# Re-ordering w_out's loads, batch 1's output and batches 2 and 3 around an expert block of an attention and gated-MLP kernel

## The chip, the cores and the metric

The kernel runs on one core of a Trainium2 chip. The core has several engines that work side by side, each through its own queue in order: TensorE (PE, matrix products, with a separate record PEld for loading weights), VectorE (DVE), ScalarE (ACT), GpSimd (POOL) and SyncE (SP, which here only issues DMAs). An instruction starts when the one before it on its engine is done and the semaphores it waits for are set. Loads are issued on POOL's queue and cast to fp16 on the way; DMA transposes and the stores are issued on SP. The metric is the device time of one execution in microseconds; lower is better. The median of three runs of the kernel before is 320.43 us (320.16 to 321.76).

## The reference, cut to what matters

```python
# q, k, v: (8 batches, 8 heads, 576 tokens, 64)
kv = einsum('bhsd,bhse->bhde', k, v)
o  = einsum('bhsd,bhde->bhse', q, kv)          # linear attention, no softmax
o  = o / sqrt(mean(o*o, axis=-1) + 1e-6) * g_norm
x  = o.transpose(0, 2, 1, 3).reshape(4608, 512)
ffn = (gelu(x @ w_gate) * (x @ w_val)) @ w_out    # w_gate, w_val: (512, 1536), w_out: (1536, 512)
out = x + sigmoid(x @ w_res) * ffn
```

Each batch is a small attention followed by an RMS norm per head; all 4608 tokens then go through a gated MLP with a gated residual. `mean(o*o)` is the sum of squares that the kernel calls `ss`, and the reciprocal of the root is its norm.

## The kernel before, in words

**Blocks and batches.** Tokens are handled in nine blocks. Block b, for b from 0 to 7, holds the first 512 tokens of batch b; block 8 holds the remaining 64 tokens of all eight. The MLP runs over d_ff in `NF` = 12 slices of 128 and over tokens in `NJ` = 4 groups of 128. `m_gval(blk, f)` computes one slice of gate and value (products of `xT`, the transposed normed tokens, with w_gate and w_val, tiles `gps` and `vps`), has ACT take the Gelu and DVE multiply the two into `hid`. For block 0 `out_by_f` multiplies `hid` with w_out slice by slice, f by f, four token groups each (`m_ffn`, tile `fps`). From block 1 on, the output is made by seven products of sums of quarters of `hid` and w_out (tiles `wA`, `wD`, `wE`, `wF`), a Strassen scheme; the sums of w_out are `wo_sums(0..3)` into `wo_ts`, those of `hid` `s_begin`, `s_rest` and `s_last`. Block 2 and later use such sums for gate and value as well (`weight_sums`, `token_sums`, tiles `Ag`, `Fg`, `Av`, `Fv`).

**Attention, one or two blocks ahead.** The attention of batch b is cut into steps which are put between pieces of the MLP of an earlier block: `load_batch` (loads of q, k, v on POOL), `by_token` (a copy of q that brings a token's heads together), `a_qT` or `d_qT` (transpose of q on PE or by DMA), `a_kv` (products of k and v into `kvp`, one copy out), `a_o` (32 small products into `op`), `a_ss` (square on ACT, reduction on DVE, one for each quarter), `a_norm` (the reciprocal root, on DVE or POOL), `a_t` (scaling `op` into `t`, DVE), `a_xT` or `d_xT` (transpose of t into `xT`, PE or DMA), and `a_g` or a scaled copy for g_norm.

**What sets the order.** The program is written out by hand: each block has a list of slots, and a dictionary `plan` from slot to steps that are issued behind it. In block 0, slots 0 to 11 are gate and value, 12 to 15 the residual gate (`m_res`, tile `rps`), 16 to 27 the output slices f = 0 to 11 (slot `NF + 4 + f`). Block 1 has `m_gval` f = 0 to 11 in slots 0 to 11, two slots of two residual products each (12 and 13), and then the seven products. `attn_plan_1` gives the steps of batch 1, which stand in block 0; `plan_attn_2` those of batch 2, in block 1; `plan_attn_ahead(b)` those of batch b in block b - 2 (batch 3 in block 1, beside batch 2). `aside_out(blk, word, ...)` puts steps between the seven products. The order on an engine is the order of issue in the program; no engine changes it.

**The loads in block 0.** Behind slot 2 POOL issues w_res, then batch 1's q, k, v and their last 64 rows (`kl`, `vl`), then w_out in four parts:

```python
load_batch(1)
for f0, f1 in ((0, 2), (2, 4), (4, 8), (8, NF)):
    load_wo(f0, f1)
```

The queue has eight DMAs in flight at most: each issue waits for the landing of one eight earlier, and the profile shows that wait before each w_out issue (1.8 to 1.9 us).

**The holds.** `load_behind(b)` issues batch b + 1's loads on POOL behind a one-element copy (tile `hold`) from the transpose of q of batch b, so that loads do not run before that transpose is done:

```python
nc.gpsimd.tensor_copy(out=hold, in_=st[b]["qT"][0:1, 0, 0, 0:1])
if x_of is not None:
    nc.gpsimd.tensor_copy(out=hold, in_=xT_t[x_of][0:1, 0, 0, 0:1])
```

Everything else that POOL has to do later waits behind that copy and the issues, the norm of batch 3 among it.

Of the kernel before, what the change touches and what calls it, by code (L numbers as in the profile page):

```python
# [18 lines left out]
def kernel(  # L19
# [96 lines left out]

    def load_batch(b):
        tiles_16(b)
        raw[b, "q"] = stage.tile([P, H, NJ * D], FP16, tag="qraw", name="qraw")
        nc.gpsimd.dma_start(out=raw[b, "q"], in_=rows4(q, b, 0, H))  # L120
        nc.gpsimd.dma_start(out=b16_t[b, "k"], in_=rows4(k, b, 0, H))
        nc.gpsimd.dma_start(out=b16_t[b, "v"], in_=rows4(v, b, 0, H))
        load_last_kv(b)
        if pair(b) is not None:
            load_qr(2 * pair(b))
            load_qr(2 * pair(b) + 1)

    def by_token(b, copy=nc.vector.tensor_copy, js=slice(0, NJ)):
# [169 lines left out]
    def a_norm(b, j0, j1, eng=nc.vector):  # L298

        s = st[b]  # L300
        if "rinv" not in s:
            s["rinv"] = attnp.tile([P, NJ + 1, H], FP32, tag="ny", name="ny")
        ss, yy = (t[:, j0:j1, :].rearrange("p j h -> p (j h)") for t in (s["ss"], s["rinv"]))
        n = (j1 - j0) * H
        m = attnp.tile([P, (NJ + 1) * H], FP32, tag="nm", name="nm")[:, 0:n]
        a = attnp.tile([P, (NJ + 1) * H], FP32, tag="na", name="na")[:, 0:n]
        mh = attnp.tile([P, (NJ + 1) * H], FP32, tag="nh", name="nh")[:, 0:n]
        magic = 0x5F1FFFF9 if eng is nc.gpsimd else 0x5F3759DF
        eng.tensor_scalar(out=m, in0=ss, scalar1=1.0 / D, scalar2=RMS_EPS, op0=ALU.mult, op1=ALU.add)
        eng.tensor_scalar(  # L310
            out=yy.bitcast(I32), in0=m.bitcast(I32), scalar1=-0.5, scalar2=float(magic), op0=ALU.mult, op1=ALU.add
        )
        if eng is nc.gpsimd:
            for step in range(2):
                eng.tensor_tensor(out=a, in0=yy, in1=yy, op=ALU.mult)
                eng.tensor_tensor(out=a, in0=a, in1=m, op=ALU.mult)
                c = (-0.703952253, 0.703952253 * 2.38924456) if step == 0 else (0.375, -1.25)
                eng.tensor_scalar(out=mh, in0=a, scalar1=c[0], scalar2=c[1], op0=ALU.mult, op1=ALU.add)
                if step == 1:
                    eng.tensor_tensor(out=mh, in0=mh, in1=a, op=ALU.mult)  # L320
                    eng.tensor_scalar(out=mh, in0=mh, scalar1=1.875, scalar2=None, op0=ALU.add)
                eng.tensor_tensor(out=yy, in0=mh, in1=yy, op=ALU.mult)  # L322
            return
        eng.tensor_scalar(out=mh, in0=m, scalar1=-0.5, scalar2=None, op0=ALU.mult)
        for _ in range(3):
            eng.tensor_tensor(out=a, in0=yy, in1=yy, op=ALU.mult)
            eng.tensor_tensor(out=a, in0=a, in1=mh, op=ALU.mult)
            eng.scalar_tensor_tensor(out=yy, in0=a, scalar=1.5, in1=yy, op0=ALU.add, op1=ALU.mult)

    def pair(b):  # L330

        return b - B // 2 if b >= B // 2 else None
# [16 lines left out]

    def a_xT(b, j):  # L350

        blk, jj = where(b, j)
        ps = pattn.tile([P, NP, P], FP16, tag="at", name="xtp")
        for cc in range(NP):
            nc.tensor.transpose(ps[:, cc, :], t_t[blk][:, jj, cc * P : (cc + 1) * P], ident)
        nc.scalar.activation(
            out=xT_t[blk][:, jj, :, :], in_=ps, func=AF.Copy, scale=gcol
        )

# [60 lines left out]

    def m_gval(blk, f, pool=pmoe, tag="mm"):
        if f == 0:
            hids[blk] = hidp.tile([P, NF, NJ * P], FP16, tag="hid", name="hid")
        gps = pool.tile([P, NJ * P], FP32, tag=tag, name="gps")
        m_mm(gps, wg_c, f, blk, 0, NJ)
        vps = pool.tile([P, NJ * P], FP32, tag=tag, name="vps")
        m_mm(vps, wv_c, f, blk, 0, NJ)
        m_act(blk, f, gps, vps)
# [491 lines left out]
    def gv_group(blk, g, banks, amid, order):  # L920
# [67 lines left out]
        for word in ORDERS[order].split():  # L988
# [12 lines left out]
            for f in amid.get(word, ()):  # L1001
                f()

    def out_by_f(blk):

# [9 lines left out]
        def step(f):  # L1015
# [3 lines left out]
            for j in range(NJ):  # L1019
                m_ffn(blk, j, f, fpss[j])  # L1020
            if NFH <= f < NFH + NJ:
                m_sigmoid(f - NFH)
# [301 lines left out]
    def attn_plan_1():  # L1324
# [11 lines left out]
                lambda: load_batch(b + 1),  # L1336
                lambda: a_kv(b),
                *[lambda j=j: a_x(0, j) for j in range(NJ)],
            ],
            NF + 4: [lambda: a_o(b), ss[0], ss[1]],  # L1340
            NF + 5: [ss[2], ss[3]],
            NF + 6: [lambda: a_norm(b, 0, NJ), t[0], t[1], t[2], t[3]],
            2 * NF: [x[0], x[1]],
            2 * NF + 1: [x[2]],
            2 * NF + 2: [x[3], lambda: wo_sums(0), lambda: wo_sums(2)],
        }
        return plan

# [20 lines left out]
    def plan_attn_2():  # L1369
# [5 lines left out]
        at(m, 3, lambda: load_behind(b))  # L1375
        at(m, 1, lambda: wo_sums(1))
        at(m, 3, lambda: wo_sums(3))
        at(m, 4, lambda: a_o(b))
        for j in range(NJ):
            at(m, 4 + j // 2, lambda j=j: a_ss(b, j))  # L1380
        at(m, 6, lambda: a_norm(b, 0, NJ, nc.gpsimd))
        for j in range(NJ):
            at(m, 9 + j // 2, lambda j=j: a_t(b, j))
        at(m, 10, lambda: d_xT(b, 0, NJ))
# [14 lines left out]
    def plan_attn_ahead(b):  # L1399
# [22 lines left out]
        else:  # L1422
            at(m, 8, lambda: by_token(b, act, slice(0, 2)))
            at(m, 9, lambda: by_token(b, act, slice(2, 4)), *begin)
            at(m, NF - 1, lambda: a_kv(b, act))
            at(m, NF, lambda: load_behind(b))
        if rem:
# [7 lines left out]
        else:  # L1435
            at(m, NF, lambda: a_o(b), lambda: a_ss(b, 0), lambda: a_ss(b, 1))
            aside_out(m, "D", lambda: a_ss(b, 2), lambda: a_ss(b, 3))
# [28 lines left out]
    sums = {u: weight_sums(u, nc.vector) for u in units}  # L1466
    for slot, u in ((2, ("g", 1)), (4, ("g", 2)), (NF - 1, ("v", 1))):
        for i in range(2):
            at(0, slot + i, *sums[u][2 * i : 2 * i + 2])
    at(0, 6, *sums["v", 2][0:2])  # L1470
    at_word(0, 0, "1v", *sums["v", 2][2:4])
    late_sums = [f for u in (("g", 0), ("v", 0)) for f in sums[u]]
    for i, f in enumerate(late_sums[0:6]):
        at(1, (2, 6, 7)[i // 2], f)
    aside_out(1, "D", *late_sums[6:8])
# [52 lines left out]
    for blk in range(B + 1):  # L1528
# [21 lines left out]
        else:  # L1550
# [27 lines left out]
            if blk == 1:  # L1578
                slots[0] = lambda: m_gval(1, 0, pattn, "at")
            outs = []  # L1580
            slots += [lambda i=i: outs[i]() for i in range(4 if blk < B else 2)]
            if not groups:
                plan.setdefault(NFH + 2, []).insert(0, lambda: s_begin(blk))

# [20 lines left out]
        for s in range(len(slots)):  # L1605
# [4 lines left out]
            if blk == 0 and s == 2:  # L1610
                nc.gpsimd.dma_start(out=wr16, in_=moe_w_res.rearrange("(cc p) c -> p cc c", p=P))
                load_batch(1)
                for f0, f1 in ((0, 2), (2, 4), (4, 8), (8, NF)):
                    load_wo(f0, f1)
# [33 lines left out]
```

## Time and profile before

| What | Value |
|---|---|
| Median of three runs | 320.43 us |
| Lowest and highest | 320.16 and 321.76 us |
| Profiled execution, device time | 321.37 us |
| Its span in the trace | 319.6 us |
| Granted PE clock, mean | 0.997 |
| PE busy | 309.9 us, 97% |
| DVE busy | 274.4 us, 86% |
| ACT busy | 210.4 us, 66% |
| POOL busy | 188.1 us, 59% |
| DMA moved | 38.89 MB |

The profiled execution is 0.94 us above the median; its span leaves out 1.77 us of its device time. A row of a timeline gives the start in us from the span's start, the duration, the engine, the line, the operation, what it writes and reads, its shape, and in brackets the idle time of the engine just before it with what ended that idle time. Rows of one kind that follow each other are joined, so "x32" are 32 instructions. Matmuls overlap their neighbours, so their durations are longer than their distances: four of 512 columns in a row are 0.865 us apart from the next four. The table of waits names, for each line of an engine, the engine or load that it waited for.

### The profile page before, as it was taken

The numbers are of one execution on the slowest core, as the hardware profiler recorded it, in microseconds if no ns is written. First come the engines' busy times: TensorE is split into PE (matmuls) and PEld (weight loads), VectorE is DVE, ScalarE is ACT, GpSimd is POOL, SyncE is SP. The second block draws the span as 40 slices with busy tenths as digits, with TensorE's granted clock in tenths as the row PEclk, the third lists the DMA queues.
The fourth block names the chain that finished last, engine by engine and source line by source line (L and its number), as shares of the span: only waits on it lengthen the run. The fifth ranks groups of instructions, "written<-read, shape, count | busy, mean of one in ns | idle before, by whom it ended". The sixth has DMA issues, their size and how long they took to land.

```text
span 319.6 us, 7763 instructions
## 1 busy us (share of the span) xinstructions
PE 309.9 (97%) x3039; PEld 246.3 (77%) x3039; DVE 274.4 (86%) x488; ACT 210.4 (66%) x385; POOL 188.1 (59%) x248
## 2 busy tenths in 40 slices
PE   8899989999999999999999999999999999999992
PEld 3544755444788888888888888888888888888882
DVE  5886979799898999989998999899988777897774
ACT  4763675455848794879587858695767467836760
POOL 2873350573769478856885888517851375396331
PEclk9999999999999999999999999999999999999998
DMA  7999999999994699479967794800540003001104
GB/s 254 327 174 198 198 200 199 177 159 184 162 130 82 199 134 111 72 216 127 108 82 216 90 143 79 216 8 0 53 162 2 0 3 134 0 2 56 77 0 131
DMA packets 77381, 38.89 MB, mean 122 GB/s; under 512 B 42274, under 2 KB 75042, under 8 KB 77346
## 3 DMA queue, kind: packets, MB, share of 16 engines
q0 software_dynamic: 39280, 17.17, 42.8%
q1 hardware_dynamic: 37488, 20.71, 25.9%
q8 instruction: 23, 0.38, 0.5%
q10 hardware_dynamic: 578, 0.52, 0.5%
q14 instruction: 12, 0.10, 0.1%
HBM read 38.80 MB, written 9.44 MB: 151 GB/s over the span
## 4 chain that ended last, share of the span: by engine, by line
PE 84%; DMA 11%; SPq 1%; POOL 1%; DVE 1%; issue 0%; DVEq 0%
PE Av L949 12%; PE Ag L949 12%; PE wA L518 11%; PE Fv L949 6%; PE Fg L949 6%; DMA wg<-in_moe_w_gate_dram 5%; DMA wo<-in_moe_w_out_dram 5%; PE rA L569 4%; PE gps L413 3%; PE fps L450 3%; PE vps L413 3%; PE Eg L949 3%; PE wF L518 3%; PE wE L518 3%; PE wD L518 3%; PE Ev L949 3%
## 5 line engine op out<-in xcount | busy, mean ns | idle before, releaser
L986 POOL TENSOR_TENSOR hid<-ge,c 128x512 f16<-128x512 f16 x22 | 25.6, 1165 | 37.3 <-ACT ge L980 35.9
L518 PEld LDWEIGHTS <-hid_s 128*128 128x128 f16 x384 | 37.6, 98 | 4.3
L364 POOL TENSOR_TENSOR t<-t,g 128x512 f16<-128x512 f16 x32 | 37.8, 1212 | 0.0
L949 PEld LDWEIGHTS <-wsv 128*128 128x128 f16 x352 | 34.1, 98 | 4.8 <-issue 0.3
L949 PEld LDWEIGHTS <-wsg 128*128 128x128 f16 x352 | 34.4, 98 | 4.0
L705 POOL TENSOR_TENSOR osb<-osb,t 128x512 f32<-128x512 f32 x28 | 34.1, 1249 | 0.0
L959 ACT COPY Eg<-Ag 128x512 f32<-128x512 f32 x22 | 12.8, 582 | 27.9 <-PE Ag L949 27.9
L518 PEld LDWEIGHTS <-hid 128*128 128x128 f16 x288 | 28.2, 98 | 3.5
L949 PEld LDWEIGHTS <-wg 128*128 128x128 f16 x264 | 25.8, 98 | 3.2
L949 PEld LDWEIGHTS <-wv 128*128 128x128 f16 x264 | 25.8, 98 | 3.0
L949 PE MATMUL Av<-ts,wsv 128*128 128x256 f16 x176 | 26.4, 272 | 0.1
L949 PE MATMUL Ag<-ts,wsg 128*128 128x256 f16 x176 | 26.4, 273 | 0.0
L970 DVE TENSOR_TENSOR Fg<-Ag,d 128x512 f32<-128x512 f32 x22 | 15.3, 696 | 11.1 <-ACT d L963 8.2
L261 DVE TENSOR_REDUCE ss<-sq 128x8 f32<-128x512 f32 x32 | 20.5, 679 | 2.3 <-ACT sq L256 2.3
L401 ACT ACTIVATE ge<-gps 128x512 f16<-128x512 f32 x20 | 11.8, 597 | 15.5 <-PE gps L413 14.8
L518 PE MATMUL wA<-wo_ts,hid_s 128*128 128x256 f16 x168 | 20.6, 272 | 0.0
L348 DVE TENSOR_TENSOR t<-op,ny 128x512 f16<-128x512 f32 x28 | 18.7, 684 | 1.0 <-POOL ny L322 0.4
L980 ACT ACTIVATE ge<-Eg 128x512 f16<-128x512 f32 x22 | 13.1, 597 | 9.2 <-PE Eg L949 9.2
L413 PE MATMUL vps<-xT,wv 128*128 128x512 f16 x72 | 18.5, 379 | 0.4 <-DMA wv<-in_moe_w_val_dram 0.3
L980 ACT ACTIVATE ge<-c 128x512 f16<-128x512 f32 x22 | 13.8, 625 | 7.7 <-DVE c L970 7.7
L413 PE MATMUL gps<-xT,wg 128*128 128x512 f16 x72 | 18.5, 379 | 0.0
L980 ACT ACTIVATE ge<-Fg 128x512 f16<-128x512 f32 x22 | 13.0, 591 | 8.3 <-PE Fg L949 6.6
(220 smaller groups left out, 852.5 us busy)
## 6 DMA issues: line engine op xcount, KB each, us to landing
out_dram<-osb SPq DMA_DIRECT2D x14, 512.0 KB, 3.8
qraw<-in_q_dram POOLq DMA_DIRECT2D x7, 512.0 KB, 6.7
k<-in_k_dram POOLq DMA_DIRECT2D x7, 512.0 KB, 8.4
v<-in_v_dram POOLq DMA_DIRECT2D x7, 512.0 KB, 11.0
wg<-in_moe_w_gate_dram POOLq DMA_DIRECT2D x2, 512.0 KB, 9.3
wo<-in_moe_w_out_dram POOLq DMA_DIRECT2D x2, 512.0 KB, 13.7
out_dram<-osb SPq DMA_DIRECT2D x4, 256.0 KB, 3.7
wv<-in_moe_w_val_dram POOLq DMA_DIRECT2D x3, 256.0 KB, 8.4
```

The source lines that it names most:

```text
L261: nc.vector.tensor_reduce(out=out_, in_=sqs.pop((b, i)), op=ALU.add, axis=mybir.AxisListType.X)
L348: nc.vector.tensor_tensor(out=t, in0=o, in1=scale, op=ALU.mult)
L364: eng.tensor_tensor(out=t_t[blk][:, jj, :], in0=t_t[blk][:, jj, :], in1=g16, op=ALU.mult)
L413: nc.tensor.matmul(ps[:, j0 * P : j1 * P], lhsT=w[:, cc, :], rhs=xT_t[blk][:, j0:j1, cc, :], start=(cc == 0 and j0 == 0), stop=(cc == NP - ...
L518: nc.tensor.matmul(ps[:, e - es[0], :], lhsT=a[:, f, e * P : (e + 1) * P], rhs=b[:, f, :], start=(start and e == es[0] and f == 0), stop=( ...
L569: nc.tensor.matmul(out_[:, e, :], lhsT=x_[:, e, cc, :], rhs=w_[:, cc, :], start=(first and e == 0 and cc == 0), stop=(cc == 1), skip_group ...
L705: nc.gpsimd.tensor_tensor(out=res_all[of], in0=res_all[of], in1=t_t[blk][of], op=ALU.add)
L949: nc.tensor.matmul(out_[:, r, :], lhsT=lhsT, rhs=rhs, start=(first and r == 0 and c == 0), stop=(c == 1), skip_group_check=True,)
L959: nc.scalar.copy(out=tile_of("E", u), in_=ps["A", u])
L970: nc.vector.tensor_tensor(out=dst, in0=ps["A", u], in1=sb["d", u], op=ALU.add)
L980: nc.scalar.activation(out=ge[q], in_=source(q, "g"), func=AF.Gelu)
L986: eng.tensor_tensor(out=dst, in0=ge[q], in1=source(q, "v"), op=ALU.mult)
```

## The change

- **w_out's loads.** Slices 0 to 2 are issued between k and v of batch 1, then slice 3, then 4 and 5, 6 to 8 and 9 to 11 behind batch 1's loads: five parts for four.
- **`load_batch`.** It takes `amid`, what to issue between k and v; the remainders' `qr` loads go ahead of k; for batch 4 the last rows of k and v are issued later, at the end of block 1's products.
- **Batch 1.** `a_kv` moves from behind the residual products to behind f = 2 of block 0's output, with its copy on ACT for DVE; `a_o` and all four `ss` go into f = 3 behind its second token group (`amid_step`); norm and `t` go behind f = 4; the four `xT` go behind f = 10 and into f = 11, the third evacuated on DVE for ACT. `wo_sums(0)` and `wo_sums(2)` leave block 0 for block 1.
- **Norm on DVE.** Nine operations with other constants instead of twelve.
- **Block 1's first `m_gval`.** Both products of f = 0 are made in two halves of 256 columns.
- **Batch 2.** `a_o` and `ss` one slot later, the norm on DVE for POOL and one slot later, `t` one slot earlier; some sums of weights in other slots; `s_begin` of block 1 in slot 10 for 8.
- **Batch 3.** `a_kv` one slot later (behind the first two residual products), `a_o` one slot later (behind all four), and batch 4's loads are held for batch 2's `xT` as well as batch 3's `qT`.

The order of DMAs on SP is the same in both kernels: batch 3's transpose of q is issued ahead of batch 2's transpose of x in both.

```diff
-    def load_batch(b):
+    def load_batch(b, amid=lambda: None):
...
-        nc.gpsimd.dma_start(out=b16_t[b, "k"], in_=rows4(k, b, 0, H))
-        nc.gpsimd.dma_start(out=b16_t[b, "v"], in_=rows4(v, b, 0, H))
-        load_last_kv(b)
         if pair(b) is not None:
             load_qr(2 * pair(b))
             load_qr(2 * pair(b) + 1)
+        nc.gpsimd.dma_start(out=b16_t[b, "k"], in_=rows4(k, b, 0, H))
+        amid()
+        nc.gpsimd.dma_start(out=b16_t[b, "v"], in_=rows4(v, b, 0, H))
+        if pair(b) != 0:
+            load_last_kv(b)
...
-        eng.tensor_scalar(out=mh, in0=m, scalar1=-0.5, scalar2=None, op0=ALU.mult)
-        for _ in range(3):
-            eng.tensor_tensor(out=a, in0=yy, in1=yy, op=ALU.mult)
-            eng.tensor_tensor(out=a, in0=a, in1=mh, op=ALU.mult)
-            eng.scalar_tensor_tensor(out=yy, in0=a, scalar=1.5, in1=yy, op0=ALU.add, op1=ALU.mult)
+        eng.tensor_tensor(out=a, in0=yy, in1=yy, op=ALU.mult)
+        eng.tensor_tensor(out=a, in0=a, in1=m, op=ALU.mult)
+        eng.scalar_tensor_tensor(out=mh, in0=a, scalar=2.38924456, in1=yy, op0=ALU.subtract, op1=ALU.mult)
+        eng.tensor_tensor(out=a, in0=mh, in1=mh, op=ALU.mult)
+        eng.tensor_tensor(out=a, in0=a, in1=m, op=ALU.mult)
+        eng.scalar_tensor_tensor(
+            out=yy, in0=a, scalar=1.25 / (0.375 * c**2), in1=a, op0=ALU.subtract, op1=ALU.mult
+        )
+        eng.scalar_tensor_tensor(
+            out=yy, in0=yy, scalar=1.875 / (0.375 * c**4), in1=mh, op0=ALU.add, op1=ALU.mult
+        )
...
-    def a_xT(b, j):
+    def a_xT(b, j, eng=nc.scalar):
...
+        if eng is nc.scalar:
+            nc.scalar.activation(out=xT_t[blk][:, jj, :, :], in_=ps, func=AF.Copy, scale=gcol)
+        else:
+            eng.tensor_scalar(out=xT_t[blk][:, jj, :, :], in0=ps, scalar1=gcol, scalar2=None, op0=ALU.mult)
...
-    def m_gval(blk, f, pool=pmoe, tag="mm"):
+    def m_gval(blk, f, pool=pmoe, tag="mm", step=NJ):
...
+        for j in range(0, NJ, step):
+            m_mm(gps, wg_c, f, blk, j, j + step)
+            m_mm(vps, wv_c, f, blk, j, j + step)
...
             for j in range(NJ):
                 m_ffn(blk, j, f, fpss[j])
+                for g in amid_step.get((f, j), ()):
+                    g()
...
                 lambda: load_batch(b + 1),
-                lambda: a_kv(b),
...
-            NF + 4: [lambda: a_o(b), ss[0], ss[1]],
-            NF + 5: [ss[2], ss[3]],
-            NF + 6: [lambda: a_norm(b, 0, NJ), t[0], t[1], t[2], t[3]],
-            2 * NF: [x[0], x[1]],
-            2 * NF + 1: [x[2]],
-            2 * NF + 2: [x[3], lambda: wo_sums(0), lambda: wo_sums(2)],
+            NF + 6: [lambda: a_kv(b, nc.scalar.copy)],
+            NF + 8: [lambda: a_norm(b, 0, NJ), *t],
+            2 * NF + 2: [x[0]],
         }
+        amid_step[3, 1] = [lambda: a_o(b), *ss]
+        amid_step[NF - 1, 1] = [x[1], lambda: a_xT(b, 2, nc.vector)]
+        amid_step[NF - 1, 3] = [x[3]]
...
-        at(m, 1, lambda: wo_sums(1))
-        at(m, 3, lambda: wo_sums(3))
-        at(m, 4, lambda: a_o(b))
+        at(m, 1, lambda: wo_sums(0), lambda: wo_sums(1))
+        at(m, 3, lambda: wo_sums(2))
+        at(m, 4, lambda: wo_sums(3))
+        at(m, 5, lambda: a_o(b))
         for j in range(NJ):
-            at(m, 4 + j // 2, lambda j=j: a_ss(b, j))
-        at(m, 6, lambda: a_norm(b, 0, NJ, nc.gpsimd))
+            at(m, 5 + j // 2, lambda j=j: a_ss(b, j))
+        at(m, 7, lambda: a_norm(b, 0, NJ))
         for j in range(NJ):
-            at(m, 9 + j // 2, lambda j=j: a_t(b, j))
+            at(m, 8 + j // 2, lambda j=j: a_t(b, j))
...
-            at(m, NF - 1, lambda: a_kv(b, act))
-            at(m, NF, lambda: load_behind(b))
+            at(m, NF, lambda: a_kv(b, act), lambda: load_behind(b, b - 1))
+            aside_out(m, "end", lambda: load_last_kv(b + 1))
...
-            at(m, NF, lambda: a_o(b), lambda: a_ss(b, 0), lambda: a_ss(b, 1))
+            at(m, NF + 1, lambda: a_o(b), lambda: a_ss(b, 0), lambda: a_ss(b, 1))
...
-    for slot, u in ((2, ("g", 1)), (4, ("g", 2)), (NF - 1, ("v", 1))):
+    for slot, u in ((2, ("g", 1)), (5, ("g", 2)), (NF - 1, ("v", 1))):
...
-    at(0, 6, *sums["v", 2][0:2])
+    at(0, 7, *sums["v", 2][0:2])
...
-        at(1, (2, 6, 7)[i // 2], f)
+        at(1, (2, 10, 11)[i // 2], f)
...
-                slots[0] = lambda: m_gval(1, 0, pattn, "at")
+                slots[0] = lambda: m_gval(1, 0, pattn, "at", NJ // 2)
...
-                plan.setdefault(NFH + 2, []).insert(0, lambda: s_begin(blk))
+                plan.setdefault(NF - 2, []).insert(0, lambda: s_begin(blk))
...
-                load_batch(1)
-                for f0, f1 in ((0, 2), (2, 4), (4, 8), (8, NF)):
+                load_batch(1, lambda: load_wo(0, 3))
+                for f0, f1 in ((3, 4), (4, 6), (6, 9), (9, NF)):
                     load_wo(f0, f1)
```

## Prediction

> **What bounds the kernel now.** I read the page's first lines, then the table of waits for PE, then PE's timeline from 41 us (w_out arrives) to 95 us, and last DVE's and POOL's timelines beside it.
>
> ```profile
> span 319.6 us, 7763 instructions
> PE 309.9 (97%) x3039; PEld 246.3 (77%) x3039; DVE 274.4 (86%) x488; ACT 210.4 (66%) x385; POOL 188.1 (59%) x248
> PEclk9999999999999999999999999999999999999998
> PE fps L450 <- DMA wo<-in_moe_w_out_dram: 0.6, 1, 0.6
> PE kvp L211 <- DMA vl<-in_v_dram: 0.3, 1, 0.3
> ```
>
> PE is busy for 97% of the span at a granted clock above 0.9. Between 38 and 60 us it has two named waits, both for loads: 0.32 us for the last rows of v, 0.56 us for w_out. Behind 83 us I find no idle PE. So a gain can come only from those waits and a few switches of matmul shape, about 1 us; and what makes PE wait later is lost whole.
>
> ```profile
> 42.39 0.22 PE L211 MATMUL kvp<-vl,kl 128*64 128x64 f16 x2 [0.32 <-DMA vl<-in_v_dram]
> 43.65 1.04 PE L450 MATMUL fps<-wo,hid 128*128 128x512 f16 x4 [0.56 <-DMA wo<-in_moe_w_out_dram]
> 44.61 0.64 PE L233 MATMUL op<-kv,qT 64*128 64x64 f16 x32
> 55.67 0.59 PE L413 MATMUL gps<-xT,wg 128*128 128x512 f16 x2
> 80.60 0.64 PE L233 MATMUL op<-kv,qT 64*128 64x64 f16 x32
> 81.17 1.90 PE L433 MATMUL rps<-wr,xT 128*128 128x512 f16 x8
> 88.15 1.47 PE L518 MATMUL wA<-wo_ts,hid_s 128*128 128x256 f16 x12
> 93.87 0.60 PE L949 MATMUL Fv<-ts,wsv 128*128 128x256 f16 x4
> ```
>
> These are PE's rows of before (start, duration, shape, idle in brackets). 55.67 is block 1's first gate and the yardstick for the first part; 80.60 is batch 3's output (`op`), 93.87 the first product that can be late through batch 3's norm.
>
> ```profile
> 85.58 1.28 DVE L261 TENSOR_REDUCE ss<-sq 128x8 f32<-128x512 f32 x2 [0.47 <-ACT sq L256]
> 87.11 0.70 DVE L481 TENSOR_TENSOR wF<-wA,wd 128x512 f32<-128x512 f32 x1 [0.25 <-PE wA L518]
> 91.34 0.69 DVE L348 TENSOR_TENSOR t<-op,ny 128x512 f16<-128x512 f32 x1 [0.39 <-POOL ny L322]
> 79.68 0.37 POOL L1356 COPY hold<-qT 1x1 f16<-1x1 f16 x1 [5.00 <-DMA qT<-q]
> 86.96 0.22 POOL L309 TENSOR_SCALAR nm<-ss 128x32 f32<-128x32 f32 x1 [1.28 <-DVE ss L261]
> 91.05 0.25 POOL L322 TENSOR_TENSOR ny<-nh,ny 128x32 f32<-128x32 f32 x1
> ```
>
> DVE's and POOL's rows: batch 3's chain of `ss` (sums of squares), norm on POOL, `t` on DVE has 0.4 to 0.5 us of slack ahead of PE, and no more.
>
> **Block 0: loads and batch 1 (until 55 us).** An issue's start plus its time to landing gives, for before: q 36.16, k 38.80, v 41.47, kl 41.91, vl 42.35, then w_out's parts 43.60, 44.89, 47.46, 50.16, q of batch 2 52.63. So 512 KB take 2.6 us, 256 KB 1.27, 64 KB 0.44, one slice of 128 rows 0.64. In the new order: slices 0 to 2 at 38.80 + 1.9 = 40.70, v 43.37, kl 43.81, vl 44.25, slice 3 44.89, 4 and 5 46.18, 6 to 8 48.1, the rest 50.1. The fifth part costs the queue nothing by these rows (bounds: 0, and one POOL issue, 0.71; I take 0, since each issue waits 1.8 to 1.9 us for an earlier landing anyway). It moves POOL's next `hid` from 37.20 to about 39.6, needed only near 51.
>
> Here a page speaks against the change: the Trainium skill, "DMA: Bandwidth & Descriptors", section "Anatomy of one DMA — SWDGE (gpsimd) path", gives each such DMA a fixed 2.0 us beside its bytes. By it slices 3 and up would land some 2 us later and the sum would be about +1.5, an estimate from that page. The landings above, 0.44 us apart for 64 KB, show no such term in a queue that is never empty.
>
> PE then goes: q's transposes end at 41.7, f=0 starts at once (before: kvp, then w_out at 43.65). Each f is 0.865 (7.08 us for 32 matmuls, pipelined, = 0.216 each). f=0 to 2 end at 44.38; kvp 0.75, its kl/vl part at 44.52 against vl 44.25; f=3 at 45.13 against 44.89; a_o inside f=3 at 45.67; f=4 46.67 against 46.18; f=6 48.40 against 48.1; f=9 50.99 against 50.1; f=10 ends 52.72. Batch 1's norm follows a_o by 3.57 us as before (44.61 to 48.18), so it starts at 49.24; nine operations of 0.226 and 0.30 to the first t: 51.34; four t of 0.6 end at 53.83. The transpose of x's third part waits for it about 0.28 us. Block 1's first gate comes at 54.76 instead of 55.67: **-0.91** (0.32 + 0.56, + 0.3 for switches of shape saved, - 0.28). Bounds: 0 (each late load eats its own margin) and 1.2 (without that wait).
>
> m_gval f=0 in halves is 16 matmuls of 256 columns for 8 of 512: by the rows 0.109 us against 0.216, nothing. The third xT evacuated on DVE (0.39 by an earlier such row) lands before the second half asks for it; its cover is the first half, 0.87 us.
>
> The Trainium skill, "TensorE: Matmul & The Clock Gate", section "Back-to-back issue gap", has a sustained 131 ns for 512 columns and 81 ns for 128, so halving would cost at least 0.25 us. Here 512 columns take 216 ns and 256 take 109, so the rows make it free.
>
> **Block 1: DVE, POOL, batches 2 and 3.** DVE takes over two sums of w_out (0.87 each) and batch 2's norm (nine operations of 0.226, 2.0 us), together 3.8 us, in a stretch from 55 to 79 us in which it idles about 4.3 us; block 1's `hid` rows then keep 0.5 to 1 us ahead of PE. Bounds: 0 and about 1 us; I take 0, as the added work is spread over five slots. POOL's norm of batch 2 was 69.81 to 74.68 (4.87 us, with waits 1.28); t(2) is done at about 76.7 and not 78.4, so xT(2)'s transpose starts 1.7 us earlier. What becomes late next is batch 3:
>
> - a_kv(3) and a_o(3) go one slot later, behind the last two residual products. PE's order becomes rps 0 and 1, kvp, rps 2 and 3, op. With the 0.91 in hand, rps starts at 77.10, and op at 77.10 + 1.74 + 0.76 + 1.74 = 81.4 instead of 80.60: 0.82 later.
> - The first reduction follows op by 1.22 (81.82 - 80.60): 82.67 instead of 81.82. From there DVE runs without a break: 1.2, s_last 0.86, weight sums 1.2 and 0.42, and the next two reductions from 85.9 to 87.2 (before 85.58 to 86.86; of the 0.85 shift 0.47 idle is swallowed). The `wF` operation, which was at 87.11 and now is wanted 0.9 earlier, starts at 87.1 to 87.2 and ends near 87.8.
> - PE's fifth product, 88.15 before, could start at 87.24 and waits for it to 87.84: of 0.91 stay 0.31.
> - The norm of batch 3 on POOL needs the last reduction: 87.27 instead of 86.96. Its own 4.34 us (86.96 to 91.30) end at 91.61, t goes at 91.65, the second t ends at 94.13 (before 91.34 and 93.82). The product Fv needs its place in PSUM: 94.18 instead of 93.87. From there PE is full in both, so **+0.31** stays.
>
> What cancels: the gain is lost at the reductions, then the norm's end sets PE. Bounds for this step: -0.91 (the chain has slack elsewhere) to +0.85 (the whole shift arrives).
>
> **POOL's queue.** Ahead of batch 4's loads it now waits also for xT(2) (a second `hold`). Queued behind it on POOL: q, qr twice, k and v of batch 4 (0.98, 1.41, 0.89, 0.90, with the copies about 4.6 us), and behind those the norm of batch 3. The last kv loads, 1.43 us, move behind it, and are needed after 109 us. The norm is undisturbed while xT(2) lands by 82.7. It is issued at about 76.7; qT's own transpose took 4.26, xT(2) 6.73 in which batch 4's loads started. Without those I take 5 us, 81.7: no cost. With 6.73: 83.4, +0.8. If it lands as before (78.45 + 6.73 = 85.18): +2.5.
>
> Nothing costs: qr's place in the order (its transpose comes after 100 us), s_begin two slots later (0.96 us on DVE, used by the second product), vl and kl of batch 4. On SP nothing is moved past anything: q's transpose of batch 3 (75.36) stood ahead of x's of batch 2 (78.45) already.
>
> **Sum.** -0.91 + 0.60 + 0.62 = +0.31 us, by the profiled execution, which took 321.37 (span 319.6 and 1.77 outside); that is 0.94 over the median of 320.43. On the median: 320.43 + 0.3 = **320.7**. About 0.5%, 1.6 us, is what a measurement of this kernel can tell from no change.
>
> **Rivals.**
> 1. The gain reaches the end. For: both losses in the sum (0.60 and 0.62) hang on slacks of 0.3 to 0.5 us, worked out by hand, on DVE and ACT. Against: no row of before shows more slack behind 85.6. Then 320.4 - 0.9 = 319.5.
> 2. Slower: POOL is held by xT(2). It decides from a landing at 83.9 on (over 1.6 us lost). For: the transpose took 6.73 us before. Against: that was beside batch 4's loads. 321.5 with the old duration, 323.2 with the old landing.
> 3. w_out's slices come late: the margins at f=3 and f=6 are 0.24 and 0.3 us. For: the landings vary by 0.1 a load. Against: nothing new shares the queue. It costs 0.3 to 0.9: 321.2.
> 4. The change does not do what it says: the order on SP is the one of before, so that part does nothing; were the rest as hidden, 320.4.
>
> **How the numbers follow.** Forecast (+0.3, own range 320.2 to 321.2) 0.48; rival 1 0.22, rival 2 0.18, rival 3 0.10, rival 4 0.02. Rival 1's floor is 320.43 - 1.2 = 319.2. Slower by over 0.5% (322.0): half of rival 2, and 0.03 of rivals 3 and the forecast's tail, 0.12. Faster by over 0.5% (318.8) lies past the idle PE that exists: 0.04. Within: 0.84. The range 319.2 to 322.2 leaves out about 0.15.
>
> **What would show it.** PE's f=0 at 41.7 with no wait for w_out, and block 1's first gate at 54.8; op of batch 3 behind all four rps at 81.4; the last reduction ending near 87.2; a wait of PE of some 0.6 us for `wF` or DVE near 87.2; batch 3's norm from 87.3 to 91.6; the holds on POOL over by 82.7. I am wrong if xT(2) lands after 83, if a w_out slice makes PE wait, if DVE's `hid` makes PE wait in block 1, or if PE is found ahead at 94 us.

## The result and the profile after

The changed kernel takes 322.15 us in the median of 22 runs (320.45 to 323.65), the kernel before, run beside it, 320.28 us (21 runs). A few runs of these kernels came at 327.7 to 331.6 us and are left out of all medians and ratios here. The ratio is 1.0053, with a 95% interval of 1.0038 to 1.0069: slower by 1.2 to 2.2 us. The time lies inside the range that was given (319.2 to 322.2), 0.05 us from its upper end; the forecast itself, 320.7, was too low by 1.45 us.

The profiled execution of the changed kernel took 321.37 us (span 319.6), 0.8 us under its own median, and by chance exactly as long as the profiled execution of the kernel before, which lay 0.9 us over its median. So the two spans cannot be compared; stretches between the same two instructions can. These are the first lines of the page of the changed kernel:

```profile
span 319.6 us, 7777 instructions
PE 310.2 (97%) x3047; PEld 247.0 (77%) x3047; DVE 276.5 (87%) x494; ACT 209.9 (66%) x385; POOL 183.7 (57%) x238
```

DVE has 2.1 us more work, POOL 4.4 us less. From the table of waits of the changed kernel for PE, the three that the kernel before does not have (us in total, times, longest):

```profile
PE Ag L966 <- ACT Eg L976: 0.7, 1, 0.7
...
PE Fg L966 <- DVE t L363: 0.4, 1, 0.4
PE wA L535 <- DVE wF L498: 0.4, 1, 0.4
```

The two waits for loads, 0.32 and 0.56 us, are gone from it. PE's timeline of the changed kernel, the rows that answer to those shown of the kernel before:

```profile
40.32 2.76 PE L467 MATMUL fps<-wo,hid 128*128 128x512 f16 x12
...
53.46 0.60 PE L429 MATMUL gps<-xT,wg 128*128 128x256 f16 x4
...
80.21 0.64 PE L235 MATMUL op<-kv,qT 64*128 64x64 f16 x32
...
86.56 1.47 PE L535 MATMUL wA<-wo_ts,hid_s 128*128 128x256 f16 x12 [0.37 <-DVE wF L498]
...
91.93 0.60 PE L966 MATMUL Fg<-ts,wsg 128*128 128x256 f16 x4 [0.41 <-DVE t L363]
93.18 0.60 PE L966 MATMUL Ag<-ts,wsg 128*128 128x256 f16 x4 [0.65 <-ACT Eg L976]
93.72 0.60 PE L966 MATMUL Fv<-ts,wsv 128*128 128x256 f16 x4
```

At block 1's first gate PE is 2.21 us ahead of the kernel before (53.46 for 55.67); 1.43 us of that it already had at q's transposes of batch 1 (39.34 for 40.77), where the kernel before itself comes at 39.32 in a second profile. At Fv it is ahead by 0.15 (93.72 for 93.87). What is lost goes at three waits between 86 and 94 us. Their idle times make 1.43 us, but a matmul's end in the profile is modelled. By the starts, the three matmuls come 0.53, 0.57 and 0.81 us later behind the ones before them than in the kernel before. DVE's timeline of the changed kernel:

```profile
81.43 1.28 DVE L263 TENSOR_REDUCE ss<-sq 128x8 f32<-128x512 f32 x2 [0.51 <-ACT sq L258]
...
84.63 1.27 DVE L263 TENSOR_REDUCE ss<-sq 128x8 f32<-128x512 f32 x2
85.82 0.69 DVE L498 TENSOR_TENSOR wF<-wA,wd 128x512 f32<-128x512 f32 x1
...
91.19 0.69 DVE L363 TENSOR_TENSOR t<-op,ny 128x512 f16<-128x512 f32 x1 [1.61 <-POOL ny L329]
91.80 0.68 DVE L718 TENSOR_TENSOR osb<-th,wF 128x512 f32<-128x512 f32 x1
```

and POOL's:

```profile
82.23 0.18 POOL L1378 COPY hold<-xT 1x1 f16<-1x1 f16 x1 [4.17 <-DMA xT<-t]
82.77 0.93 POOL L120 DMA_DIRECT2D qraw<-in_q_dram  x1 [0.36 <-issue]
...
85.90 0.93 POOL L126 DMA_DIRECT2D v<-in_v_dram  x1
86.90 0.24 POOL L314 TENSOR_SCALAR nm<-ss 128x32 f32<-128x32 f32 x1
...
90.90 0.25 POOL L329 TENSOR_TENSOR ny<-nh,ny 128x32 f32<-128x32 f32 x1
```

Read together: batch 3's reductions end at 85.90 (84.63 and 1.27). The norm could start there, but POOL stands at the hold on xT until 82.41, issues five loads, and starts the norm at 86.90. No idle time is shown in front of it: that is the mark of a queue and not of a wait. DVE's t waits 1.61 us for the norm's end, and behind t in DVE's order stands `osb<-th,wF`, which needs nothing of batch 3; ACT's copy Eg needs the place in PSUM that it frees, and PE waits 0.65 us for Eg. (In this profile Eg's wait is put down to PE's Fg, which ended 0.05 us behind that piece; in those of "no hold on xT" and "both undone" below it is put down to the piece.)

All further readings go by one table: PE's time in us between the starts of its first q transpose of batch 1, block 1's first gate, the first of the seven products, the second-block Fv, and the last matmul, in one profiled execution each. "Batch 3 early" means its output as in the kernel before.

| Kernel | q to gate | gate to product | product to Fv | Fv to last | q to last |
|---|---|---|---|---|---|
| before | 14.89 | 27.24 | 10.96 | 219.79 | 272.89 |
| before, second profile | 15.27 | 27.25 | 10.95 | 219.70 | 273.17 |
| changed | 14.12 | 27.32 | 12.94 | 219.96 | 274.34 |
| changed, second profile | 14.25 | 27.32 | 12.89 | 219.95 | 274.41 |
| no hold on xT | 13.97 | 27.32 | 12.13 | 219.93 | 273.36 |
| batch 3 early | 14.22 | 28.51 | 11.30 | 219.94 | 273.97 |
| both undone | 14.11 | 27.33 | 11.53 | 219.96 | 272.93 |
| block 0's part alone | 14.02 | 28.84 | 10.95 | 220.06 | 273.86 |
| batch 3's part alone | 15.01 | 27.23 | 15.15 | 220.33 | 277.72 |
| both undone, t behind wF's piece | 13.96 | 27.33 | 10.93 | 219.95 | 272.18 |

The changed kernel gains 0.6 to 1.2 us before the gate, loses 1.95 between the first product and Fv, 0.1 before it, and 0.2 later (at 140 us two matmuls come 0.07 and 0.17 us late that do not in the kernel before). That makes 1.2 to 1.5 us, and the runs' 1.2 to 2.2 fit it.

### The profile page after: what moved, and what is told of

Its sections match the earlier page's. It is cut to its first block, busy times and chain, and to the rows that moved or that the text cites. A ratio compares the mean times of both kernels' runs of the same rounds, so it can differ in the third digit from the quotient of the medians.

```text
span 319.6 us, 7777 instructions
## 1 busy us (share of the span) xinstructions
PE 310.2 (97%) x3047; PEld 247.0 (77%) x3047; DVE 276.5 (87%) x494; ACT 209.9 (66%) x385; POOL 183.7 (57%) x238
## 4 chain that ended last, share of the span: by engine, by line
PE 85%; DVE 5%; DMA 3%; POOL 2%; issue 1%; SPq 1%; ACT 0%; DVEq 0%; POOLq 0%
PE Av L966 12%; PE Ag L966 12%; PE wA L535 10%; PE Fv L966 6%; PE Fg L966 6%; PE gps L429 4%; PE vps L429 4%; PE rA L586 4%; PE Ev L966 3%; PE Eg L966 3%; PE w L535 2%; PE wD L535 2%; PE wF L535 2%; PE wE L535 2%; DMA xT<-t 2%; PE rF L586 2%
## 5 line engine op out<-in xcount | busy, mean ns | idle before, releaser
L429 PE MATMUL gps<-xT,wg 128*128 128x512 f16 (+1 forms) x76 | 18.7, 368 | 0.0
L429 PE MATMUL vps<-xT,wv 128*128 128x512 f16 (+1 forms) x76 | 18.6, 368 | 0.0
```

Of the source, the lines that this page charges most:

```text
L429: nc.tensor.matmul(ps[:, j0 * P : j1 * P], lhsT=w[:, cc, :], rhs=xT_t[blk][:, j0:j1, cc, :], start=(cc == 0 and j0 == 0), stop=(cc == NP - ...
```

## The experiments

Each kernel below starts from the changed one unless it is said otherwise, and is timed beside the kernel before, whose median in the three groups was 320.25, 320.43 and 320.45 us. The kernels of the first four headings are of the first group.

### The changed kernel again

> The changed kernel once more, for a second profile beside the kernels of this group. Theory A (POOL's second hold, on batch 2's xT, keeps POOL busy with batch 4's loads until after batch 3's last reduction): the two transposes land one behind the other, xT about 4.35 us behind qT (82.23 - 77.88 in the first profile), POOL comes free 4.6 us behind the hold and later than the end of batch 3's last reduction, and the norm starts there. About 322.1 us. Theory B (batch 3's output behind all four residual products is what makes the norm late): the norm starts within 0.2 us of the last reduction's end, the holds are over before.

No edit. 321.58 us in the median, ratio 1.0039 (1.0023 to 1.0055). Theory A's picture: the hold on xT at 83.12, POOL through with the loads at 87.71, the norm at 87.79, without idle time, 0.95 us behind the last reduction's end (85.57 and 1.27). xT landed 4.5 us behind qT (83.00 and 78.48).

### Without the hold on batch 2's xT

```diff
-            at(m, NF, lambda: a_kv(b, act), lambda: load_behind(b, b - 1))
+            at(m, NF, lambda: a_kv(b, act), lambda: load_behind(b))
```

> The changed kernel with the hold on batch 2's xT taken out, nothing else. Theory A: POOL is free before batch 3's last reduction, the norm starts 0.9 us earlier against PE's own order (86.0 for 86.9 in the first profile's times) and the time falls by 0.6 to 0.9 us from the changed kernel, to about 321.3. Batch 4's loads then run beside xT's transpose, which lands up to 1 us later. Theory B: no difference, within 0.2 us. A third way (the hold was there to keep the loads off the transpose, and xT now comes late for DVE's scaling by g): slower by 0.5 us or more.

321.20 us, ratio 1.0023 (1.0007 to 1.0039), 0.4 us under the changed kernel of the same group, which by the runs alone could be chance. The traces decide more. POOL's timeline of this kernel:

```profile
78.44 0.18 POOL L1376 COPY hold<-qT 1x1 f16<-1x1 f16 x1 [10.79 <-DMA qT<-q]
...
82.46 0.93 POOL L126 DMA_DIRECT2D v<-in_v_dram  x1
86.68 0.21 POOL L314 TENSOR_SCALAR nm<-ss 128x32 f32<-128x32 f32 x1 [3.29 <-DVE ss L263]
```

POOL now idles 3.29 us ahead of the norm and waits for the reduction. From the first product to Fv it takes 12.13 us for 12.9: the hold costs 0.8 there. Theory A is right for that part, and the hold bought nothing here that PE would need: xT landed at 81.27, 5.1 us behind its issue, and DVE's scaling of it (87.09) did not wait. But 1.2 us of the loss remain.

### Batch 3's output early, hold kept

```diff
-            at(m, NF, lambda: a_kv(b, act), lambda: load_behind(b, b - 1))
+            at(m, NF - 1, lambda: a_kv(b, act))
+            at(m, NF, lambda: load_behind(b, b - 1))
...
-            at(m, NF + 1, lambda: a_o(b), lambda: a_ss(b, 0), lambda: a_ss(b, 1))
+            at(m, NF, lambda: a_o(b), lambda: a_ss(b, 0), lambda: a_ss(b, 1))
```

> The changed kernel with batch 3's a_kv and a_o back where the kernel before has them (ahead of the residual products and between them); the hold on xT stays. Theory A: PE's wait of about 0.4 us for wF goes, but the norm still starts when POOL comes free, so the time stays within 0.3 us of the changed kernel, about 322. Theory B: the whole loss goes, 1.2 us or more, to 320.9 or less.

322.24 us, ratio 1.0059 (1.0039 to 1.0079). Not theory B: the loss does not go. PE's wait for wF is gone and the norm still starts directly behind the loads (87.65), as theory A said. In place of the wait for wF stands one that neither theory had foreseen, in PE's timeline of this kernel:

```profile
80.96 0.64 PE L235 MATMUL op<-kv,qT 64*128 64x64 f16 x32 [1.11 <-DMA qT<-q]
```

Batch 3's q transpose landed 6.4 us after its issue, where the kernel before has 4.3 and 4.4. In the eleven profiles of kernels with block 0's part of the change it landed after 4.3 to 4.5 us in eight and after 6.4 to 6.7 in three. A late output does not wait for that: in the first kernel of "The copy of q and the fifth load" below, q's transpose landed after 6.5 us and PE did not wait at `op`. An early one does.

### Both undone

The two edits above together.

> The changed kernel without the hold on xT and with batch 3's a_kv and a_o back in their places. Theories A and B both: PE's three waits between 85 and 94 us (0.37 + 0.41 + 0.65 = 1.43 us in the first profile) go, 1.3 us or more under the changed kernel, about 320.8; if the first part's gain (1.2 us from q's transposes of batch 1 to block 1's first gate) holds in every run, 319.2, under the kernel before. A third way: what is lost lies elsewhere, and the time stays at 322.

320.65 us, ratio 1.002 (0.9995 to 1.0046): 0.9 us under the changed kernel of the group, with intervals that overlap. From the kernel with the early output it differs by the hold alone and is 1.6 us faster; those two intervals overlap by little (1.0039 to 1.0046). Two of PE's three waits are gone. DVE's timeline, and ACT's and PE's rows that follow from it, show the third:

```profile
89.85 0.69 DVE L363 TENSOR_TENSOR t<-op,ny 128x512 f16<-128x512 f32 x1 [0.90 <-POOL ny L329]
90.46 0.68 DVE L718 TENSOR_TENSOR osb<-th,wF 128x512 f32<-128x512 f32 x1
```

```profile
91.22 0.57 ACT L976 COPY Eg<-Ag 128x512 f32<-128x512 f32 x1 [4.68 <-DVE osb L718]
```

```profile
91.84 0.60 PE L966 MATMUL Ag<-ts,wsg 128*128 128x256 f16 x4 [0.35 <-ACT Eg L976]
```

From q's transposes to the last matmul it takes as long as the kernel before (272.93 for 272.89 and 273.17). So the gain in block 0 is eaten even here, by 0.57 us between the first product and Fv and 0.2 later.

### The parts by themselves

Block 0's part alone is the kernel "both undone" with batch 2's norm on POOL and block 1's sums (weights, `s_begin`, `a_o(2)`) in their old slots; two sums of w_out stay in block 1:

```diff
-        at(m, 7, lambda: a_norm(b, 0, NJ))
+        at(m, 6, lambda: a_norm(b, 0, NJ, nc.gpsimd))
...
-        at(1, (2, 10, 11)[i // 2], f)
+        at(1, (2, 6, 7)[i // 2], f)
...
-                plan.setdefault(NF - 2, []).insert(0, lambda: s_begin(blk))
+                plan.setdefault(NFH + 2, []).insert(0, lambda: s_begin(blk))
```

> The kernel before with block 0's part of the change only (w_out's five parts and their places, batch 1's output inside f = 3, its norm and transposes, the two halves of block 1's first slice, two sums of w_out moved into block 1); batch 2's norm on POOL, the sums of weights in block 1, and batch 3 as before; the last rows of batch 4's k and v at the end of block 1 as in the change. Theory C (what is left of the loss in the run before this, with hold and batch 3 undone, is DVE's added work in block 1, the norm of batch 2 and the sums that were pushed to its last slots): 0.5 us under that run, 319.6 to 320.1, with no wait of PE at 84 to 94 us. Rival: the gain of block 0 is not there in an ordinary run of the kernel before, because its wait for w_out is smaller there; then 320.3 and the stretch from q's transposes to block 1's first gate about equal in both.

320.44 us, ratio 1.0003 (0.998 to 1.0025): no difference from the kernel before. The chain behind the products is whole again (10.95 us), so theory C is right that DVE's added work in block 1 is what kept "both undone" at 11.53. The late `op` of this run does not explain it: DVE idled 2.18 us ahead of batch 3's first reduction, more than the 1.29 us that PE waited, where in "both undone" it had no idle time there. But the profiled run had batch 3's q transpose late (6.7 us), and PE waited 1.29 us for it ahead of `op`. Where that run lost the gain is shown; that the others did so too is not.

Batch 3's part alone, on the kernel before:

```diff
-            at(m, NF - 1, lambda: a_kv(b, act))
-            at(m, NF, lambda: load_behind(b))
+            at(m, NF, lambda: a_kv(b, act), lambda: load_behind(b, b - 1))
...
-            at(m, NF, lambda: a_o(b), lambda: a_ss(b, 0), lambda: a_ss(b, 1))
+            at(m, NF + 1, lambda: a_o(b), lambda: a_ss(b, 0), lambda: a_ss(b, 1))
```

> The kernel before with batch 3's part only: a_kv and a_o one slot later and the hold of batch 4's loads on batch 2's xT as well. Theory A: xT lands about 4.3 us behind qT (qT at 79.6 in the profile of before, so 83.9 or up to 85.2), POOL comes free 4.6 us later, at 88.5 to 89.8, and batch 3's norm starts there instead of 86.96: slower than before by 1.5 to 2.8 us, 321.8 to 323.1. Theory B (only the late output counts): the reductions end 0.4 us later, slower by 0.4 to 0.5 us, 320.7.

325.19 us, ratio 1.014 (1.0106 to 1.0173), worse than theory A's upper bound. POOL's timeline, then PE's:

```profile
83.85 0.92 POOL L1358 COPY hold<-xT 1x1 f16<-1x1 f16 x1 [4.77 <-DMA xT<-t]
84.71 0.98 POOL L120 DMA_DIRECT2D qraw<-in_q_dram  x1
...
88.99 1.39 POOL L100 DMA_DIRECT2D qr<-in_q_dram  x2
90.45 0.21 POOL L309 TENSOR_SCALAR nm<-ss 128x32 f32<-128x32 f32 x1
```

```profile
95.02 1.01 PE L949 MATMUL Fg<-ts,wsg 128*128 128x256 f16 x4 [2.34 <-DVE t L348]
```

The norm starts 4.6 us behind its place in the kernel's second profile (90.45 for 85.88, with the q transposes 0.4 apart). Here the last rows of k and v stand ahead of the norm as well, so POOL needs 6.6 us from the hold to the norm, and 4.7 in the changed kernel. Of the 1.9 us between these two, 1.57 are the issues of the last rows (87.42 to 88.99), which the changed kernel has moved behind the norm. Without the rest of the change the hold is by far the most expensive step, since theory B's estimate for the late output alone was 0.4 to 0.5 us; neither was run by itself on the kernel before.

### t behind wF's output piece

"Both undone", with

```diff
-            aside_out(m, "01" if m + 1 == WHOLE else "11", *first[0:2])
+            aside_out(m, "11", *first[0:2])
```

> The kernel with hold and batch 3's output undone, and besides t of batch 3's first quarter on DVE behind block 1's third output piece (osb<-th,wF) instead of ahead of it. If ACT's copy Eg, which follows that output piece, is late because the piece stands behind t, and t waits 0.90 us for POOL's norm: the piece runs at 88.9 instead of 90.46, PE's wait of 0.51 us for Eg goes, and the time falls by 0.4 to 0.6 us under the kernel with both undone, to 320.1 or 320.2. If t itself (its place in PSUM) sets PE, no change.

The chain does what was expected: the output piece runs at 89.52 instead of waiting behind t, PE's timeline shows no wait between 41 and 98 us, and from q's transposes to the last matmul it takes 272.18 us, 0.7 to 1.0 under the kernel before. The runs do not show it: 320.76 us, ratio 1.0007 (0.9987 to 1.0026), between 319.35 and 322.72. The profiled run took 320.0 and shows where it lost 0.66 us ahead of that stretch. DVE's, POOL's and PE's timelines of this kernel:

```profile
37.78 2.33 DVE L131 COPY q<-qraw 128x2048 f16<-128x2048 f16 x1
```

```profile
37.60 0.76 POOL L162 DMA_DIRECT2D wo<-in_moe_w_out_dram  x1 [1.92 <-DVE wsv L498]
38.38 1.18 POOL L1003 TENSOR_TENSOR hid<-ge,c 128x512 f16<-128x512 f16 x1
```

```profile
40.17 1.07 PE L192 MATMUL qtp<-ident,q 128*128 128x128 f16 x16 [0.66 <-DVE q L131]
```

The copy of q takes 0.68 or 0.69 us in twelve of the fourteen profiles, 2.32 in that without the hold, and 2.33 here. It ends 0.55 us behind POOL's `hid` (38.38 and 1.18 make 39.56).

### The kernel before again

> The kernel before once more, for a second profile. If the first one (321.37 us, 0.9 over the median) was late through slow loads at the start, q's transposes of batch 1 come at 39.3 to 39.8 instead of 40.77, and the stretch from there to block 1's first gate is 14.9 us or somewhat more, as PE then waits longer for w_out; the time about 320.3.

320.30 us. q's transposes come at 39.32, the loads are waited for as in the first profile:

```profile
40.59 0.32 PE L211 MATMUL kvp<-v,k 128*64 128x64 f16 x8 [0.21 <-DMA v<-in_v_dram]
41.25 0.22 PE L211 MATMUL kvp<-vl,kl 128*64 128x64 f16 x2 [0.35 <-DMA vl<-in_v_dram]
42.57 1.04 PE L450 MATMUL fps<-wo,hid 128*128 128x512 f16 x4 [0.63 <-DMA wo<-in_moe_w_out_dram]
```

So the gain that the change can take away is 1.2 us here, and the first profile's 0.9 us over the median lay at the start (q's transposes 1.45 us later).

### The copy of q and the fifth load

```diff
-            NF - 1: [lambda: by_token(b)],
+            NF - 2: [lambda: by_token(b)],
```

> The changed kernel with DVE's copy of batch 1's q ahead of the first pair of value sums instead of behind it. Theory D (the fifth w_out issue and the hid operation that it pushes back occupy POOL from 37.6 to 39.6 us, and a DVE instruction that starts in that time does not get going until POOL is done: the copy of q took 2.3 us for 0.68 in two of seven profiles, the sum behind it 1.8 to 2.0 for 0.42 in the five others): the copy is done by 37.6 us against q's transposes at 39.3, PE never waits for it, q to block 1's first gate takes 14.0 to 14.3 us, some sum takes 1.8 us in its place, and the time falls by 0.1 to 0.3 us on average, to about 321.6. Without theory D: no change and copies of 2.3 us go on.

321.51 us, ratio 1.0037 (1.0019 to 1.0055); against the changed kernel the difference is within the runs' spread. The copy took 0.69 us, and the first sum of the second pair behind it 2.01. Its profiled run was a long one (322.67 us): q's transpose landed late, the hold on xT was passed at 84.09, and from product to Fv it took 13.68 us.

```diff
-                for f0, f1 in ((3, 4), (4, 6), (6, 9), (9, NF)):
+                for f0, f1 in ((3, 5), (5, 8), (8, NF)):
```

> The changed kernel with w_out in four parts (0 to 2, 3 and 4, 5 to 7, 8 to 11), nothing else. Theory D: without the fifth issue POOL's hid stands 2 us or more earlier, no DVE copy or sum between 36 and 42 us takes more than 0.7 us. In exchange f = 3 waits 0.4 to 0.7 us for slices 3 and 4 (256 KB behind vl, 1.27 us, for 128 KB, 0.64). Time 321.5 to 322.3. If long DVE operations stay, the fifth issue is not their cause.

322.51 us, ratio 1.0073 (1.0051 to 1.0096), a little more than was expected. PE waits 0.62 us at f = 3, as worked out. From the first product to Fv it takes 13.67 us: the hold on xT was passed only at 84.28, so in this run, as in the one above, the hold cost 1.5 us and not 0.8. On DVE every long operation between 36 and 42 us is gone (the longest takes 0.69 us):

```profile
37.97 0.69 DVE L131 COPY q<-qraw 128x2048 f16<-128x2048 f16 x1
38.57 0.42 DVE L498 TENSOR_TENSOR wsv<-wv 128x512 f16<-128x512 f16 x1
```

POOL's last w_out issue and `hid` run from 35.34 to 37.30. That supports theory D: the fifth issue, and `hid` right behind it, stand among DVE's copies and sums. Which of the two does the holding up, this run does not separate.

### Two ways to keep the gain

The kernel of "t behind wF's output piece" with the copy of q first:

> The kernel with hold and batch 3's output undone and t behind wF's output piece, and besides the copy of q first as above. From q's transposes to the end 272.2 us as before it, no wait for the copy; 0.2 to 0.4 us under it, 320.4. Runs in which batch 3's q transpose lands late (6.4 to 6.7 us for 4.4, two of four profiles with the early output) still cost up to 1.3 us, so the spread stays over 1.5 us.

320.41 us, ratio 0.999 (0.9971 to 1.0009), from 319.21 to 321.80. The profiled run is the fastest of all, 319.21 us, with no wait in PE's timeline from 34 to 98 us and 272.20 us from q's transposes to the last matmul.

The changed kernel without the hold, with the copy of q first, t behind the output piece, and

```diff
-            at(m, NF + 1, lambda: a_o(b), lambda: a_ss(b, 0), lambda: a_ss(b, 1))
-            aside_out(m, "D", lambda: a_ss(b, 2), lambda: a_ss(b, 3))
+            at(m, NF + 1, lambda: a_o(b), *[lambda j=j: a_ss(b, j) for j in range(NJ)])
...
-    aside_out(1, "D", *late_sums[6:8])
...
-    aside_out(1, "D", wr_[3])
+    aside_out(1, "22", *late_sums[6:8], wr_[3])
```

> The changed kernel made to keep its gain: batch 3's output stays late (so that it never waits for q's transpose), no hold on xT, all four reductions of batch 3 directly behind the output, the last sums of weights behind wF, t behind wF's output piece, copy of q first. If the three causes (hold, reductions behind other DVE work, output piece behind t) are all of the loss: first product to Fv 10.9 to 11.0 us as in the kernel before, q's transposes to the end 272.2 us, 0.8 us or more under the kernel before (319.5), and a narrower spread. If DVE's added work is itself the limit, wF or Fg wait and it stays at 320.4.

320.22 us, ratio 0.9994 (0.9971 to 1.0017), from 319.82 to 322.11, product to Fv 11.59. The norm no longer waits for anything late, but the sums of weights that were moved now stand ahead of another output piece, and PE waits for that:

```profile
89.16 1.47 PE L535 MATMUL wA<-wo_ts,hid 128*128 128x256 f16 x12 [0.50 <-DVE osb L498]
```

Neither can be told from the kernel before by its runs.

## Why the prediction was right and wrong

**The bound, and block 0.** Right. The gain was forecast as 0.91 us to block 1's first gate; from q's transposes it measures 0.77 against the first profile of before and 1.15 against the second. f = 0 followed q's transposes at once, and no slice was late, though the margin at f = 3 was 0.04 us (landed 43.81, used 43.85) and not 0.24. The halves cost 0.08 us at most (the first slice took 53.46 to 55.27, 1.81 us for 8 times 0.216), not the 0.25 us that was estimated from the section "Back-to-back issue gap" of the Trainium skill's "TensorE: Matmul & The Clock Gate". Slice 3, 128 KB, landed 0.69 us behind vl.

**"The fifth part costs the queue nothing."** True of the queue and wrong of the kernel. The step asked when POOL's next `hid` is needed and not what it meets where it goes: a DVE copy or sum that starts while POOL issues the last part takes 1.3 to 1.7 us longer and ends just behind `hid`. Mostly that hits a sum off PE's path; in two of the seven profiles with five parts and the copy in its old place it hit the copy of q, and PE waited 0.65 us.

**Batch 3's output late.** The mechanism was right, place by place: `op` behind all residual products, the reductions without a break, then PE's wait for wF (0.60 worked out, 0.53 by the starts), then t, then Eg. The two losses of the sum, 0.60 and 0.62, make 1.22 us, and without the hold the stretch from product to Fv does lose 1.18. That so much of it fits is luck: late against early output, both without the hold, is only 0.60, and the rest is DVE's added work, which the sum had at 0 (below).

**The hold on xT: the step that failed.** The text took "5 us, 81.7: no cost" for xT's landing and kept 6.73 us, 83.4 and +0.8 as a rival. It landed 6.2 and 5.9 us after its issue in the two profiles of the changed kernel, and the hold cost 0.8 us, which is the rival's figure. The issue came late as well. DVE's and SP's timelines of the changed kernel:

```profile
74.10 1.28 DVE L363 TENSOR_TENSOR t<-op,ny 128x512 f16<-128x512 f32 x2
```

```profile
73.24 2.56 SPq L393 DMA_TRANSPOSE qT<-q  x1
```

t(2) is done at 75.38, 21.92 us behind block 1's first gate, as forecast (76.7 and 54.76 make 21.94). But the transpose of x is issued at 75.89: SP is still at q's transpose until 75.80. In the second profile it comes 0.75 us behind t(2). In the kernel before, x's transpose was issued 0.03 us behind t(2), since t(2) was the later of the two. So "on SP nothing is moved past anything" was true and no reason for a cost of nothing: the earlier t(2) met a queue that was still busy. Counted from the gate, xT landed at 28.65 and 28.60 us, where the forecast had 26.94, and 27.94 for its limit of 82.7. The 5 us came from the thought that batch 4's loads, which began beside the transpose, had made it 6.73. In the changed kernel no load of batch 4 is issued before it lands (82.11 against 82.77, 83.00 against 83.66), and it takes about 6 us all the same; the row that was there, 6.73, was the better price. The text's limit of 82.7 and its sign of being wrong, a landing after 83, were also times in the old timeline; the norm's place moves with PE, and in a run that is 1.4 us ahead the limit moves too. So the landings at 82.11 and 83.00 were not past that sign and cost time all the same. With 0.8 in place of 0, the sum is +1.1 us, and the runs gave 1.2 to 2.2. The time fell inside the range, by 0.05 us, because the range had room for the second rival, and not because the sum was right.

**"t goes at 91.65", and the piece behind it.** The forecast had the late t, but as part of batch 3's late output, and not the output piece behind it. "Both undone" and "t behind wF's output piece" show it as a cause of its own: with the output early and no hold it still cost 0.57 us, since DVE's added work (batch 2's norm, two sums of w_out, late sums) had used up the slack, and the piece stood behind a t that waited. "Bounds: 0 and about 1 us; I take 0" for DVE's added work was too low by that. It set 3.8 us of added work against about 4.3 us of idle time between 55 and 79 us; in the trace of before DVE is busy for 20.8 of these 24.0 us, which leaves 3.2.

**The rivals.** The first (the gain reaches the end) did not come about in the changed kernel; the two kernels with t behind wF's piece show it in their profiles (272.18 and 272.20 us from q's transposes to the last matmul) and not in their medians. The second is what came, at a landing earlier than the 83.9 that it named. The third did not come about with five parts. The fourth's point, that SP's order is the same, holds in all traces.

**What stays open.** Why batch 3's q transpose lands 2 us late in three of eleven profiles; what batch 3's late output costs without the hold and without DVE's added work, which was not run; and which runs of the improved kernels lose the 0.7 to 1.0 us that their profiled runs gain. Only one run of each has a trace, q's transposes of batch 1 come anywhere from 39.3 to 40.8 us in the profiles, and the landing of batch 3's q transpose adds up to 1.3 us.

## What to carry to other kernels

Charge a wait in an in-order queue with everything behind it, and count it to the point where the engine comes free in the new timeline, not to the point where the wait ends. Before an earlier input is booked as an earlier transfer, look at what the issuing queue is doing then. Where an engine moves ahead of a chain that had no slack, look for the instruction that needs nothing of the chain but stands behind one that does: moving that one took the 0.6 us out of the profile here, with the chain as slow as before. And one more load on a compute engine's queue is also one more shift of that engine's own work: ask whose instruction it will meet.

## What the runs showed of the hardware

A DVE copy from SBUF to SBUF (fp16 128x2048) took 2.33 us instead of 0.68, and a sum of two SBUF tiles 1.7 to 2.0 instead of 0.42, when POOL was issuing a load (0.76) and then running a multiplication of two SBUF tiles (1.18). The Trainium skill, "SBUF — State Buffer", section "Who interferes with whom", says that DVE and GpSimd hold a shared pair of ports for a whole instruction, and that the one that starts second waits. The traces fit that only if the load's issue counts as the one that starts first, since copy and sums all started before `hid`. The same section describes loads issued on GpSimd as held up by DVE; here it is the other way round as well. The copy of q had started at 37.78, 0.6 us before `hid` (38.38), which is about its whole length, and still ended 0.55 us behind `hid`; so the load's issue at 37.60 seems to have held it up already. It is not so in each case: in "both undone" the copy started at 37.85, 0.06 us behind the issue (37.79), took its usual 0.68, and the issue took 0.99 for 0.76.

Batch 2's DMA transpose of x landed 4.9 to 7.9 us after its issue in the fourteen profiles: 5.5 to 6.3 in the six in which no load of batch 4 was issued before it landed (6.2 and 5.9 in the changed kernel), and 4.9 to 7.9 in the eight with such loads beside it (5.1 without the hold, 4.9 in the last version, 7.9 with both undone). The times with loads spread more widely, but they are not all later.
